# The first 36 products of q in a gated attention/MLP kernel: 128 rows at once, or 64 and 64

## The chip, the cores and the metric

The kernel runs on one core of one Trainium2 chip, in one launch. The metric is the device time of that launch in microseconds (us); three runs of the kernel before gave a median of 392.82 us.

## The reference

For 2048 positions x of width 448 the reference adds two branches, weighted by a gate of each position. One branch is a dilated sliding attention (16 heads of 28, the current position and seven earlier ones at a distance of 2, 4, ... 14); the other is an MLP with a squared ReLU.

```
g   = sigmoid((x * gate_w).sum(-1))
qkv = x @ wqkv                                   # 2048x448 @ 448x1344
a   = attention(q, k, v; 8 positions, step 2) @ wo
h   = relu(x @ w1 + b1) ** 2                     # 448 -> 1792
b   = h @ w2 + b2                                # 1792 -> 448
out = g * a + (1 - g) * b
```

## The kernel before

Everything comes in as float32. The products are made in the format F32R: each matrix is split into a high part (a copy in that format, by ScalarE as a rule) and a low part (the difference, by VectorE as a rule), and each product is made three times: high by high, high by low, low by high. In the names, `wqh` and `wql` are the two parts of the weights of q, k and v, and `x.h[k]` and `x.l[k]` those of the input; k counts three blocks of 128 of the 448 contracted rows. The remaining 64 rows have tiles of their own: `x.x7` and `x.x8` are the high and the low part of the input there, `w7h` and `w7l` those of the weights.

The input comes in four chunks of 512 positions, each of four tiles of 128. A tile of q is an accumulator of 128x450 in one bank of PSUM (448 columns, and two for the gate). The tile of x is the stationary operand of a product, so each product has a weight load (PEld) of 128 columns and a matmul (PE) of 450 columns.

Nearly all products of the kernel are made in **pairs with 64 rows each** by `side_by_side` (line 351): of two products with different accumulators, one takes rows 0 to 63 of both operands and the other rows 64 to 127, and the two run at the same time. An accumulator receives both halves of its products, first in one half of the rows and later in the other. The kernel never lets two products in different halves run on one accumulator at the same time: each change of half is preceded by a tiny write of another engine (`turn`, `touch`): the write waits for the last product in the old half, and the first product in the new half waits for the write.

The exception is the beginning. `qkv_first` works on the four tiles of q of chunk 0 (`q[0]` to `q[3]`) while the input still arrives. There the 3 blocks x 3 products x 4 tiles = 36 products (line 439) use all 128 rows at once and need no turn. Each product is issued when its operands are due: block 0 goes by tiles (0, 1), then (2, 3), since x's first block arrives in two halves of 256 columns; blocks 1 and 2 go by all four tiles. Then follow the products of q with 64 rows (`last`), in pairs with those of the first tiles of k, and everything after them is pairs.

The order of each engine is fixed when the program is built: a planner (`Plan`) keeps a clock of TensorE and places the jobs of ScalarE, VectorE, GpSimd and SyncE's DMA queue by their costs and dependencies. The splits of the first operands (lines 846 to 861) are written out by hand ahead of it, and GpSimd has nothing to do there: after some small fills of constants it is idle until the attention begins.

Of the kernel before, what the change touches and what calls it, by code (L numbers as in the profile page):

```python
# [14 lines left out]
P = 128  # L15
# [8 lines left out]
NQ = D + 2  # L24
# [160 lines left out]
def gated_mix_kernel(ctx: ExitStack, tc: tile.TileContext, xT, wqkv, w1, w2, wo, b1, b2, out):  # L185
    nc = tc.nc

    def f32(ap):
        return ap.bitcast(F32)

    def woven(w):

        if w.shape[1] in (NQ, NQ + 1):
            n = NH if w.shape[1] == NQ else D // 2
            return bass.AP(tensor=w.tensor, offset=w.offset, ap=[list(w.ap)[0], [1, n], [NG, 2]])
        return w.rearrange("p (i n) -> p n i", i=2)
# [9 lines left out]
    def woven_out(pt, n):  # L206
        return (pt[:, :2 * NH] if n == NQ else pt[:, :n]).rearrange("p (n i) -> p n i", i=2)
# [85 lines left out]
    def x_tiles(c):  # L293
        if c % 2:
            x_place[0] = xpool.tile([P, 8 * CH + 16], F32R, tag="x", name=f"x{c}")
            return [x_slot(j, 0 if c == 1 else 16) for j in range(4)]
        return [xap.tile([P, 2, CH], F32R, tag=f"x{j}", name=f"x{c}_{j}") for j in range(4)]
# [28 lines left out]
    def block(b):  # L326
        o = (0, NP, NP + D)[b]
        return slice(o, o + ncols(b))
# [66 lines left out]
    def wqj(b, k):  # L395
        return wq_jobs.get((b, k), ())

    def full(x, acc, tl, b, ks=range(3)):
        sl, n = slice(tl * P, tl * P + P), block(b)
        r = []  # L400
        for k in ks:
            (wh, wl), (xh, xl) = wqj(b, k) or (None, None), x.parts[k] or (None, None)
            r += [(acc, x.h[k][:, sl], wqh[:, k, n], *filter(None, (wh, xh))),
                  (acc, x.h[k][:, sl], wql[:, k, n], *filter(None, (wl,))),
                  (acc, x.l[k][:, sl], wqh[:, k, n], *filter(None, (xl,)))]
        return r

    def last(x, acc, tl, b):
        sl = slice(tl * P, tl * P + P)
        n = block(1) if b == 2 else slice(0, NQ + b)  # L410
        h, l = w7h[:, n], w7l[:, n]
        (wh, wl), (xh, xl) = (wqj(2, 3) if b == 2 else ()) or (None, None), x.parts[3] or (None, None)
        return [(acc, x.x7[:, sl], h, *filter(None, (wh, xh))), (acc, x.x7[:, sl], l, *filter(None, (wl,))),
                (acc, x.x8[:, sl], h, *filter(None, (xl,)))]

    def accs(c, b, tls, tags):
        return [Acc(t, f"qkv{c}_{tl}_{b}", ncols(b)) for t, tl in zip(tags, tls)]

    def run(c, todo, steps):
        a = 0  # L420
        for e, done, *turns in steps:
            side_by_side(todo[0][a:e], todo[1][a:e])
            a = e
            for t in turns:
                t() if callable(t) else turn(*t)
            for b, tl, acc in done:
                assert acc.todo == 0
                qkv_evacuate(acc, c, tl, b)

    def qkv_first(x):  # L430
        four = range(4)
        q = accs(0, 0, four, "bbbb")
        for k in range(3):
            todo = [full(x, q[i], i, 0, (k,)) for i in four]
            for some in ((0, 1), (2, 3)) if k == 0 else (four,):
                for j in range(3):
                    for i in some:
                        acc, a, w, *_ = todo[i][j]
                        nc.tensor.matmul(woven_out(acc.pt, NQ), a, woven(w), start=k == j == 0, stop=False)  # L439
            plan.pe(FIRST[k])  # L440
        for acc in q:
            acc.todo = 3
        k = accs(0, 1, four, "mmmm")
        t = [sum((last(x, a[i], i, b) for i in four), []) for b, a in ((0, q), (1, k))]
        f = [full(x, k[i], i, 1) for i in four]
        run(0, [t[0] + f[0] + f[1] + f[2] + f[3], t[1] + f[2] + f[3] + f[0] + f[1]],
            [(3, [(0, 0, q[0])], (k[0], k[0])),
             (12, [(0, i, q[i]) for i in (1, 2, 3)], (k[1], k[1])),
             (24, [], (k[0], k[2])), (33, [], (k[1], k[3])),
             (39, [(1, 0, k[0]), (1, 2, k[2])]), (48, [(1, 1, k[1]), (1, 3, k[3])])])  # L450
        v = accs(0, 2, four, "bbbb")
        f, l = [full(x, v[i], i, 2) for i in four], [last(x, v[i], i, 2) for i in four]
        run(0, [f[0] + l[0] + f[2] + l[2] + f[1] + f[3], f[1] + l[1] + f[3] + l[3] + f[0] + f[2]],
            [(15, [], (v[0], v[1])), (24, [], (v[2], v[3])),
             (33, [(2, 0, v[0]), (2, 1, v[1])]), (42, [(2, 2, v[2]), (2, 3, v[3])])])
# [386 lines left out]
    x = X(x_tiles(0))  # L842
# [88 lines left out]
    for c in range(4):  # L931
        x = xs[c]
        plan.emit(*(p[0] for p in x.parts if p))
        if c == 0:
            qkv_first(x)
        else:
            qkv_two(x, c, 0)
            if c == 1:
                end = plan.t + 63 * MM448
                plan.quiet = end - 500.0, end + QUIET  # L940
            qkv_two(x, c, 2, (mlp_one, mlp_two) if c == 3 else ())
        chunk_done(c)
# [298 lines left out]
    rows = wo_d.rearrange("(i b) n -> i b n", b=14)  # L1241
# [31 lines left out]
    for g in range(2, 2 * NF):  # L1273
        i, f = g // (NF // 2), g % (NF // 2) * 2
# [3 lines left out]
        last = g == 2 * NF - 1  # L1278
        if not f:
            x, slots = X([nxt[j][0] for j in range(4)]), [nxt[j][1] for j in range(4)]  # L1280
# [105 lines left out]
```

## Time and profile before

| | |
|---|---|
| median of three runs | 392.82 us (392.77 to 393.04) |
| the profiled execution, its own time | 392.98 us |
| its span in the profile | 391.0 us (so 1.98 us lie around it) |
| PE, busy share of the span | 99% |
| DVE, ACT, POOL | 68%, 53%, 67% |
| granted TensorE clock | 1.00 |

PE is TensorE's matmul, PEld its weight load, DVE VectorE, ACT ScalarE, POOL GpSimd and SP the queue that issues most DMAs. An instruction's row in the timeline gives its start and length in us; rows that follow each other on one line of the kernel are merged, and xN says how many there are. A matmul's length holds its way through the array, so successive matmuls overlap: the distance between starts is what a product costs in a stream. In a pair the two starts are a few ns apart.

### The profile page before, as it was taken

Reading aid. Unit: us, or ns where it says so; the run is one execution under the profiler, and the core shown is the slowest. Engines: PE = TensorE matmul, PEld = TensorE weight load, DVE = VectorE, ACT = ScalarE, POOL = GpSimd, SP = SyncE. Lnnn points to the kernel's source line nnn. Section 1 sums busy time; section 2 is a strip of 40 time slices with the busy share of each in tenths; the row PEclk is TensorE's granted clock in tenths of the full one; section 3 lists DMA queues with packets and bytes.
Section 4 is the critical chain, followed back from the end, with each engine's and each line's share of the span. In section 5 each row is a group of like instructions: output and inputs, shape, how many; then the busy total and the mean of one; then the engine's idle time right before and its main releaser. Section 6 shows DMA issues by size and latency. Waiting matters only on the chain.

```text
span 391.0 us, 9281 instructions
## 1 busy us (share of the span) xinstructions
PE 386.6 (99%) x3828; PEld 381.2 (97%) x3828; DVE 267.5 (68%) x356; ACT 205.6 (53%) x501; POOL 260.5 (67%) x165
## 2 busy tenths in 40 slices
PE   9999999999999999999999999999999999999996
PEld 8999999999999999999999999999999999999995
DVE  4525522588686778878866999789767686668454
ACT  4757866362566666445555445345716343456740
POOL 0000002988999989869899987999997979661000
PEclk9999999999999999999999999999999999999999
DMA  7999999997174062644203779745645120226835
GB/s 234 398 360 308 368 377 337 375 383 254 49 246 157 1 219 80 220 171 161 90 2 135 241 190 292 224 109 138 173 153 171 80 96 2 88 62 166 147 101 189
DMA packets 64842, 73.75 MB, mean 189 GB/s; under 512 B 32481, under 2 KB 57633, under 8 KB 64417
## 3 DMA queue, kind: packets, MB, share of 16 engines
q1 hardware_dynamic: 64368, 72.79, 57.2%
q8 instruction: 30, 0.49, 0.5%
q10 hardware_dynamic: 432, 0.38, 0.3%
q14 instruction: 12, 0.09, 0.1%
HBM read 45.71 MB, written 28.25 MB: 189 GB/s over the span
## 4 chain that ended last, share of the span: by engine, by line
PE 99%; DVE 0%; DVEq 0%; issue 0%
PE b L351 33%; PE h L351 32%; PE qkv L351 23%; PE a L351 7%; PE qkv L439 2%; PE warm L820 1%; PE a L1176 1%; DVE bt_b L1057 0%; DVEq L1381 0%
## 5 line engine op out<-in xcount | busy, mean ns | idle before, releaser
L549 POOL TENSOR_TENSOR pp<-q,k 128x896 f32<-128x896 f32 x56 | 116.7, 2119 | 77.2 <-DMA k<-k_d 64.7
L561 POOL TENSOR_TENSOR pp<-lg,v 128x896 f32<-128x896 f32 x64 | 113.8, 1868 | 7.4 <-DVE o L571 3.7
L351 PE MATMUL h<-x,w1h 64*128 64x512 f32 x672 | 114.3, 376 | 0.0
L351 PE MATMUL qkv<-wqh,x 64*128 64x448 f32 (+1 forms) x528 | 82.2, 349 | 0.0
L553 DVE TENSOR_REDUCE lg<-pp 128x32 f32<-128x896 f32 x64 | 66.9, 1076 | 13.4 <-POOL pp L549 13.2
L351 PEld LDWEIGHTS h<-x,w1h 64*128 64x128 f32 x672 | 70.9, 186 | 2.3
L806 DVE TENSOR_TENSOR h<-h,h 128x512 fp32r<-128x512 f32 x56 | 38.6, 689 | 46.7 <-ACT h L805 46.5
L571 DVE TENSOR_REDUCE o<-pp 128x112 f32<-128x896 f32 x64 | 67.8, 1070 | 0.2 <-POOL pp L561 0.2
L351 PE MATMUL h<-x,w1l 64*128 64x512 f32 x336 | 67.6, 376 | 0.0
L351 PE MATMUL b<-w2bh,h 64*128 64x448 f32 x448 | 66.6, 349 | 0.0
L351 PE MATMUL b<-w2ah,h 64*128 64x448 f32 x448 | 66.5, 349 | 0.0
L351 PEld LDWEIGHTS qkv<-wqh,x 64*128 64x128 f32 x528 | 57.3, 186 | 0.0
L802 ACT ACTIVATE h<-h,b1z 128x512 f32<-128x512 f32 x56 | 36.7, 655 | 36.8 <-PE h L351 36.8
L351 PE MATMUL qkv<-wql,x 64*128 64x448 f32 (+1 forms) x264 | 53.4, 349 | 0.0
L351 PEld LDWEIGHTS b<-w2ah,h 64*128 64x128 f32 x448 | 46.5, 193 | 0.2
L351 PEld LDWEIGHTS b<-w2bh,h 64*128 64x128 f32 x448 | 46.4, 193 | 0.2
L351 PE MATMUL b<-w2al,h 64*128 64x448 f32 x224 | 41.9, 349 | 0.0
L351 PE MATMUL b<-w2bl,h 64*128 64x448 f32 x224 | 41.9, 349 | 0.0
L351 PEld LDWEIGHTS h<-x,w1l 64*128 64x128 f32 x336 | 35.6, 186 | 1.0
L804 ACT ACTIVATE h<-h 128x512 fp32r<-128x512 f32 x56 | 33.5, 598 | 1.6
L373 ACT ACTIVATE st<-qkv 128x448 f32<-128x448 f32 x48 | 24.4, 540 | 17.1 <-PE qkv L351 12.5
L805 ACT ACTIVATE h<-h 128x512 f32<-128x512 f32 x56 | 33.2, 592 | 0.0
(112 smaller groups left out, 542.8 us busy)
## 6 DMA issues: line engine op xcount, KB each, us to landing
v<-v_d SPq DMA_DIRECT2D x8, 840.0 KB, 6.1
x_d<-x SPq DMA_DIRECT2D x12, 512.0 KB, 7.7
x<-x_d SPq DMA_DIRECT2D x12, 512.0 KB, 3.7
k<-k_d SPq DMA_DIRECT2D x7, 840.0 KB, 7.0
q_d<-st SPq DMA_DIRECT2D x8, 448.0 KB, 6.5
k_d<-st SPq DMA_DIRECT2D x8, 448.0 KB, 6.1
v_d<-st SPq DMA_DIRECT2D x8, 448.0 KB, 6.6
o_d<-o SPq DMA_DIRECT2D x16, 224.0 KB, 2.2
```

The source lines that it names most:

```text
L351: nc.tensor.matmul(woven_out(acc.pt, acc.n), a[rows], woven(w[rows]), start=acc.todo == acc.all, stop=acc.todo == 1)
L373: nc.scalar.activation(st[0][:, :, t % 2].rearrange("p (i g) c -> p i g c", i=2), unwoven(pt[:, :D]).rearrange("p i (g c) -> p i g c", c=C ...
L439: nc.tensor.matmul(woven_out(acc.pt, NQ), a, woven(w), start=k == j == 0, stop=False)
L549: nc.gpsimd.tensor_mul(pr.rearrange("p (w c) -> p w c", w=W), q[:, s:s + 1].to_broadcast([P, W, C]), k[:, s:s + W])
L553: nc.vector.tensor_reduce(lgs[i][:, s], pr.rearrange("p (w h d) -> p w h d", w=W, h=HG), axis=AX.X, op=ALU.add)
L561: nc.gpsimd.tensor_mul(pr.rearrange("p (h d w) -> p w h d", h=HG, w=W), lgs[i][:, s][:, :, :, None].to_broadcast([P, W, HG, DH]), vs[i][:, ...
L571: nc.vector.tensor_reduce(o_t[par, s][:, g * C:(g + 1) * C], pr.rearrange("p (c w) -> p c w", w=W), axis=AX.X, op=ALU.add)
L802: a = add(ACT, 656.0, lambda pt=pt, r=r: nc.scalar.activation(pt, pt, AF.Relu, bias=b1t[:, f + r:f + r + 1]), ready, *bias_job[:2], prio=NEXT)
L804: b = add(ACT, 600.0, lambda pt=pt, hh=hh: nc.scalar.activation(hh, pt, AF.Square), a, prio=NEXT)
L805: a = add(ACT, 600.0, lambda pt=pt: nc.scalar.activation(pt, pt, AF.Square), b, prio=NEXT)
L806: low = add(DVE, 690.0, lambda pt=pt, hh=hh, hl=hl: nc.vector.tensor_sub(hl, pt, f32(hh)), a, prio=NEXT)
L820: nc.tensor.matmul(warm[:, :2 * P].rearrange("p (i n) -> p i n", i=2), zero, zeros, start=True, stop=True)
```

## The change

The 36 products with 128 rows become 36 pairs with 64 rows. For each block k, a first pass makes the three products of tiles (0, 1), then those of (2, 3), each product on one half of its rows; a second pass does the same with the other halves, beginning with the product of `x.l[k]`. `r` says which half a tile is in: neighbours are in different halves, a tile changes between the passes, and from one block to the next it stays.

Between the passes GpSimd copies two columns of `x.l[k]` onto themselves (one of each tile), for tiles (0, 1) and for (2, 3): the copy waits for the first pass's products of these tiles, and the second pass waits for the copy. After the second pass of block 2 it does the same with `x.h[2]` and then `x.x8`. These are ten copies of 128x2. Since q's tiles 1 and 3 end in the half that `last` uses, they come first there, each with the product of `x.x8` ahead of the other two; q's tiles so finish in the order 1, 0, 3, 2.

```diff
         for k in range(3):
             todo = [full(x, q[i], i, 0, (k,)) for i in four]
-            for some in ((0, 1), (2, 3)) if k == 0 else (four,):
-                for j in range(3):
-                    for i in some:
-                        acc, a, w, *_ = todo[i][j]
-                        nc.tensor.matmul(woven_out(acc.pt, NQ), a, woven(w), start=k == j == 0, stop=False)
+            for second in (False, True):
+                for some in ((0, 1), (2, 3)):
+                    for j in (2, 0, 1) if second else (0, 1, 2):
+                        for i in some:
+                            acc, a, w, *_ = todo[i][j]
+                            r = (i + k + second) % 2
+                            rows = slice(r * 64, r * 64 + 64)
+                            nc.tensor.matmul(woven_out(acc.pt, NQ), a[rows], woven(w[rows]), start=k == j == 0 and not second, stop=False)
+                    if not second or k == 2:
+                        for l in (x.h[k], x.x8) if second else (x.l[k],):
+                            t = l.rearrange("p (t n) -> p t n", n=P)[:, some[0]:some[0] + 2, 0:1]
+                            nc.gpsimd.tensor_copy(t, f32(t))
             plan.pe(FIRST[k])
...
-        t = [sum((last(x, a[i], i, b) for i in four), []) for b, a in ((0, q), (1, k))]
+        t = [sum((last(x, a[i], i, b) for i in o), []) for b, a, o in ((0, q, (1, 0, 3, 2)), (1, k, four))]
+        t[0] = sum((t[0][i + 2:i + 3] + t[0][i:i + 2] for i in range(0, 12, 3)), [])
...
-            [(3, [(0, 0, q[0])], (k[0], k[0])),
-             (12, [(0, i, q[i]) for i in (1, 2, 3)], (k[1], k[1])),
+            [(3, [(0, 1, q[1])], (k[0], k[0])),
+             (12, [(0, i, q[i]) for i in (0, 3, 2)], (k[1], k[1])),
```

On TensorE's queue, the program before has the following rows at the place where block 0 ends and block 1 begins; `qkv_2_0` is tile 2 of q, `x_0` and `x_1` are the tiles of x of blocks 0 and 1 (both parts), and the words in brackets name the engines that a row waits for.

```order
L439 MATMUL qkv_2_0_197<-wqh,x_0_171 128x450 [waits DVE_49]
L439 MATMUL qkv_3_0_198<-wqh,x_0_171 128x450
L439 MATMUL qkv_0_0_195<-wqh,x_1_172 128x450 [waits Activation_49]
L439 MATMUL qkv_1_0_196<-wqh,x_1_172 128x450
L439 MATMUL qkv_2_0_197<-wqh,x_1_172 128x450
```

In the changed program the same two products of `x_0` are followed by the second pass of block 0, and block 1 comes behind it.

```order
L442 MATMUL qkv_2_0_197<-wqh,x_0_171 128x450 [waits DVE_49]
L442 MATMUL qkv_3_0_198<-wqh,x_0_171 128x450
L442 MATMUL qkv_0_0_195<-wqh,x_0_171 128x450 [waits Pool_49]
L442 MATMUL qkv_1_0_196<-wqh,x_0_171 128x450
L442 MATMUL qkv_0_0_195<-wqh,x_0_171 128x450
L442 MATMUL qkv_1_0_196<-wqh,x_0_171 128x450
L442 MATMUL qkv_0_0_195<-wql,x_0_171 128x450
L442 MATMUL qkv_1_0_196<-wql,x_0_171 128x450
L442 MATMUL qkv_2_0_197<-wqh,x_0_171 128x450 [waits Pool_49]
```

What moved is the beginning of block 1, by six pairs; two new waits for GpSimd stand ahead of it.

GpSimd's queue gets these rows, between the fills of constants and the attention; `x_2` is the tile of block 2 and `x_3` that of the last 64 rows.

```order
L446 CAST x_0_171<-x_0_171 128x2 [waits DVE_49,PE_49] x2
L446 CAST x_1_172<-x_1_172 128x2 [waits DVE_49,PE_49]
L446 CAST x_1_172<-x_1_172 128x2 [waits PE_49]
L446 CAST x_2_173<-x_2_173 128x2 [waits DVE_49,PE_49]
L446 CAST x_2_173<-x_2_173 128x2 [waits PE_49]
L446 CAST x_2_173<-x_2_173 128x2 [waits PE_49,Activation_49]
L446 CAST x_3_174<-x_3_174 128x2 [waits DVE_49]
L446 CAST x_2_173<-x_2_173 128x2 [waits PE_49]
L446 CAST x_3_174<-x_3_174 128x2
```

Nothing else of GpSimd moved. On ScalarE, VectorE and SP the instructions stand as before, apart from q's tiles, which leave PSUM in the order 1, 3, 0, 2 where it was 0, 2, 1, 3.

## The prediction, made before the changed kernel ran

> **What bounds the kernel now.** I read the page first (busy time, then the chain that ended last), then TensorE's waits:
>
> ```profile
> PE 386.6 (99%) x3828; PEld 381.2 (97%) x3828; DVE 267.5 (68%) x356; ACT 205.6 (53%) x501; POOL 260.5 (67%) x165
> PE 99%; DVE 0%; DVEq 0%; issue 0%
> PE b L351 33%; PE h L351 32%; PE qkv L351 23%; PE a L351 7%; PE qkv L439 2%; PE warm L820 1%; PE a L1176 1%; DVE bt_b L1057 0%; DVEq L1381 0%
> ...
> PE warm L820 <- PEq L1378: 0.8, 1, 0.8
> ```
>
> The chain is 99% TensorE, and its only wait is for the start of the program. So the end moves by what the start of the stream of products moves, one to one: what the changed 2% (L439) loses or gains stands at the end. What follows shows how tight that part is, first TensorE itself:
>
> ```profile
> 4.95 1.05 PE L439 MATMUL qkv<-wqh,x 128*128 128x450 f32 x2
> 5.83 0.56 PE L439 MATMUL qkv<-wql,x 128*128 128x450 f32 x2
> 6.22 0.92 PE L439 MATMUL qkv<-wqh,x 128*128 128x450 f32 x4
> ...
> 12.11 0.35 PE L439 MATMUL qkv<-wqh,x 128*128 128x450 f32 x1
> 12.39 0.46 PE L351 MATMUL qkv<-w7h,x 64*128 64x450 f32 x2
> ...
> 12.69 0.35 PE L351 MATMUL qkv<-w7l,x 64*128 64x450 f32 x2
> 12.88 0.54 PE L351 MATMUL qkv<-w7h,x 64*128 64x450 f32 x4
> ```
>
> From the fifth product (6.22) to the 36th (12.11) there are 31 distances in 5.89 us: 0.19 each. Pairs with 64 rows also come every 0.19 (12.69 to 12.88). So 36 products cost as much as 36 pairs. Two things are lost beside that. The first products are slow: three by 5.83, about 0.37 each. And at the change from 128 to 64 rows the next pair should start at 12.11 + 0.19 = 12.30, but the second one stands at 12.69, as if the first had run from 12.50: 0.20 lost. I take 12.50 as the true start of that pair (below: the 37th).
>
> The operands come from VectorE (low parts) and ScalarE:
>
> ```profile
> 4.72 0.69 DVE L853 TENSOR_TENSOR wql<-wqraw,wqh 128x225 fp32r<-128x225 f32 x2
> 5.32 0.42 DVE L857 TENSOR_TENSOR x<-xraw,x 128x256 fp32r<-128x256 f32 x1
> 6.07 0.43 DVE L857 TENSOR_TENSOR x<-xraw,x 128x256 fp32r<-128x256 f32 x1 [0.33 <-ACT x L856]
> 6.54 0.63 DVE L847 TENSOR_TENSOR wql<-wqraw,wqh 128x450 fp32r<-128x450 f32 x1
> 7.08 0.68 DVE L857 TENSOR_TENSOR x<-xraw,x 128x512 fp32r<-128x512 f32 x1
> 7.69 0.62 DVE L847 TENSOR_TENSOR wql<-wqraw,wqh 128x450 fp32r<-128x450 f32 x1
> 8.66 0.69 DVE L857 TENSOR_TENSOR x<-xraw,x 128x512 fp32r<-128x512 f32 x1 [0.35 <-ACT x L856]
> 9.82 0.63 DVE L859 TENSOR_TENSOR w7l<-wqraw,w7h 128x450 fp32r<-128x450 f32 x1 [0.47 <-ACT w7h L858]
> 10.64 0.69 DVE L861 TENSOR_TENSOR x<-xraw,x 128x512 fp32r<-128x512 f32 x1 [0.19 <-ACT x L860]
> 11.25 1.74 DVE L269 TENSOR_TENSOR wql<-wqraw,wqh 128x448 fp32r<-128x448 f32 x3
> ...
> 5.62 0.42 ACT L856 ACTIVATE x<-xraw 128x256 fp32r<-128x256 f32 x1 [0.91 <-DMA xraw<-xT]
> ```
>
> **The change, part by part.** *The drain.* The change from 128 to 64 rows moves from 12.3 to the first product, where TensorE waits for operands anyway: at most 0.20 gained.
>
> *Operands that are due earlier.* How soon does a product follow the write of its operand? A cast, the weight load of the first product, and that of the 37th pair:
>
> ```profile
> 4.52 0.28 DVE L851 CAST x<-xraw 128x256 fp32r<-128x256 f32 x1
> ...
> 4.92 0.50 PEld L439 LDWEIGHTS qkv<-wqh,x 128*128 128x128 f32 x2 [0.25 <-ACT wqh L849]
> 12.39 0.19 PEld L351 LDWEIGHTS qkv<-w7h,x 64*128 64x128 f32 x2 [0.28 <-ACT wqh L266]
> ```
>
> The weight load of 4.92 starts 0.12 after the cast's end (4.80), with two waits; and behind the load of 12.39 the pair's true start (12.50) is 0.11 later. I take 0.09 + 0.11 = 0.20. The first pair stays at about 5.1 and the second at 5.5. Pair 3 needs x.l[0]'s first half (5.74): 5.94. Pair 4 needs x.h[0]'s second half (ScalarE, 6.04): 6.24. Pair 6 needs x.l[0]'s second half (6.50): 6.70. Before, these came as the 5th, 7th and 11th product and cost no wait. Pair 7 can start at 6.89, and with no further wait pair 37 at 6.89 + 30 x 0.19 = 12.59, against 12.50. So the drain's 0.20 is given back whole to later operands: **+0.09**, and 0.00 would need a reaction 0.1 quicker.
>
> *The GpSimd copies, if they were alone.* How soon does one follow? Rows:
>
> ```profile
> 13.30 0.16 ACT L358 ACTIVATE qkv<-b1z 1x1 f32<-1x1 f32 x1 [0.96 <-PE qkv L351]
> ...
> L251 POOL MEMSET mask<- x7: 88/91/94, 0.9 to 1.2; 1x7 f32 x1, 1x6 f32 x1, 1x5 f32 x1, 1x4 f32 x1
> ...
> L249 POOL MEMSET mask<- x1: 152/152/152, 0.7 to 0.7; 128x64 f32 x1
> ...
> L598 POOL TENSOR_TENSOR lg<-lg,mask x8: 633/656/678, 93.0 to 321.7; 128x256 f32<-128x256 f32 x8
> ```
>
> ScalarE's touch starts at 13.30, 0.07 after the third pair ended (12.88 + 0.35); I take 0.07 for GpSimd. A copy of 2 elements is bounded by 0.09 (a fill of 7) and 0.66 (256 elements, two inputs); it is nearest to the fills, and I take 0.12. The last pair of a group of three runs 0.35; then 0.07 + 0.12, then 0.20 to the next product: 0.74, against the 0.76 that the three pairs of the other tiles and itself give. So alone the copies just fit; each 0.1 more would cost about 0.1 at four places (three blocks and the end).
>
> *The GpSimd copies beside VectorE.* They are not alone. Where GpSimd worked and VectorE subtracted two SBUF tensors, this is what stands there:
>
> ```profile
> 80.42 8.18 DVE L711 TENSOR_TENSOR w2al<-w2raw,w2ah 128x1792 fp32r<-128x1792 f32 x1 [0.83 <-ACT w2ah L709]
> 89.53 1.54 DVE L711 TENSOR_TENSOR w2al<-w2raw,w2ah 128x1344 fp32r<-128x1344 f32 x1
> ...
> 78.44 4.16 POOL L549 TENSOR_TENSOR pp<-q,k 128x896 f32<-128x896 f32 x2
> 82.56 4.16 POOL L549 TENSOR_TENSOR pp<-qk 128x896 f32<-128x896 f32 x2
> 89.68 3.36 POOL L549 TENSOR_TENSOR pp<-qk 128x896 f32<-128x896 f32 x1 [2.96 <-DVE lg L553]
> ```
>
> A POOL product alone takes about 2.10 (4.16 for two that overlap a little). The one at 89.68 took 3.36 and ended at 93.04; less 2.10, it really began at 90.94, 0.13 before the end of VectorE's subtraction (89.53 + 1.54 = 91.07). And VectorE's subtraction of 80.42 stood 8.18 us until GpSimd's run was over. So the two exclude each other, whole instruction by whole instruction. In the window of the change VectorE does nothing but such subtractions, with few gaps. Walking it through, with the lock free 0.13 before a subtraction's end:
> - Block 0, tiles (0, 1): pair 3 ends at 6.29; the copy is due at 6.36, and the subtraction of 6.07 lets go at 6.37: 6.49, no loss.
> - Block 0, tiles (2, 3): pair 6 ends at 7.05, due at 7.12, but the subtraction of 7.08 has it until 7.64. Copy done at 7.76, pair 10 at 7.96 instead of 7.46: **+0.50**.
> - Block 1: pair 15 ends at 9.26, copied by 9.45 in the gap before 9.82, no loss. Pair 18 ends at 9.83, due at 9.90, and 9.82 holds it until 10.32: pair 22 at 10.64 instead of 10.24, **+0.40**.
> - Block 2: pair 27 ends at 11.94, due at 12.01; the second of the three subtractions (about 11.79 to 12.41) holds it until 12.28: pair 31 at 12.60 instead of 12.35, **+0.25**. The second copy waits for the third of them: **+0.05**.
> - The last copies (x.h[2], then x.x8) follow at 13.40 with VectorE idle: two in a row, **+0.05**. VectorE's next block hangs on ScalarE behind a touch that waits for pair 39, so it moves along.
>
> Sum: 0.09 + 0.50 + 0.40 + 0.25 + 0.05 + 0.05 = **1.34 us**. Against the profiled execution's own time: 392.98 + 1.34 = 394.32; that execution lies 0.16 above the median, so 392.82 + 1.34 = **394.2**.
>
> Here a rule can be set beside the row of 8.18. The Trainium skill, "SBUF — State Buffer", section "Who interferes with whom", says that a GpSimd instruction that reads SBUF and a VectorE instruction with two SBUF inputs contend, and that whichever issues first holds the port for its whole instruction. By it, one subtraction is waited for, and the sum stays as above. The row says more: VectorE was passed over between three successive GpSimd instructions. If that holds the other way round, it is the first rival.
>
> *VectorE's own delay* by the copies is at most 0.12 each, and the products that need its operands come later than that; nothing. *q's other order:* three tiles are evacuated after the same steps as before; nothing. SP's stores of x now also wait for the copies, and what is queued behind them would be held up; but the first of them comes ten us after the last copy (about 14):
>
> ```profile
> 23.70 3.26 SPq L885 DMA_DIRECT2D x_d<-x  x3
> ```
>
> So nothing. From there on every engine follows TensorE's stream, so they move along by the same amount.
>
> **The rivals.**
> 1. *GpSimd is passed over between back-to-back subtractions*, as VectorE was. Then the copy due at 7.12 waits out 7.08 and 7.69 (until 8.31 - 0.13 = 8.18): pair 10 at 8.50, +1.04. The later stalls shift: +0.43 at block 1 (until 10.32), +0.26 at block 2, +0.10 at the end. Sum with 0.09: 1.92, so 394.7. For it: the row of 8.18. Against it: no row shows GpSimd passed over; at 89.68 it got in behind one subtraction.
> 2. *No exclusion for so small a copy, so no slower:* two elements slip in, the copies fit in 0.76, and only the operands' +0.09 stays: 392.9. It holds as long as a copy comes out of GpSimd within 0.14 of its start. For it: nothing but the size. Against it: 89.68 waited before it did any work.
> 3. *Quicker reactions and the drain saved*: pair 3 at 5.83 and no wait after it: pair 37 at 5.83 + 34 x 0.19 = 12.29, a gain of 0.21: 392.6. Against it: x.l[0] ends at 5.74 and 6.50.
> 4. *Something dearer*: a copy of 0.3 or more on top of the exclusion adds 0.2 at four places and makes 395 and above.
>
> **How the numbers follow.** A measurement of this kernel can tell about 0.2%, 0.79 us, from no change: the bounds are 392.0 and 393.6. Forecast 0.47 (1.0 to 1.7 with the luck of who comes first at 7.1, 9.8 and 12.0); rival 1 0.22, rival 2 0.24, rival 3 0.03, rival 4 0.04. Slower by over 0.2%: 0.47 + 0.22 + 0.04 = 0.73. Within: 0.24 + 0.02 = 0.26. Faster by that much: 0.01, as even rival 3 stays inside. The range reaches from rival 2 (392.9) past rival 1 (394.7), with 0.2 for unknown lengths of a copy: 392.9 to 394.9.
>
> **What would show it.** In the changed profile: pairs 4 and 6 near 6.2 and 6.7; a hole of about 0.5 in TensorE's starts between 7.3 and 8.0 (of 1.0 for rival 1), another near 10.3 and 12.5; TensorE waiting for POOL at L442; POOL's copies of 0.1, but of 0.4 to 0.6 where VectorE subtracts; the first pair of `last` at 13.8 instead of 12.5; and from there all as before, shifted by 1.3. It is wrong if the copies run at 0.1 to 0.15 beside VectorE's subtractions, or if TensorE's shift at 14 us is not the shift at the end.

## The result, and the profile after

| | before | changed |
|---|---|---|
| median of six runs each, same chip | 392.88 us | 394.75 us (394.64 to 395.05) |
| ratio | | 1.0049, 95% interval 1.0036 to 1.0062 |
| profiled execution, own time / span | 392.98 / 391.0 us | 394.64 / 392.8 us |

The change made the kernel 1.87 us slower. The forecast was 394.2 with a range of 392.9 to 394.9; a second comparison of the same two kernels on another chip (below) gave 1.50.

The page of the changed kernel: busy time, and the chain that ended last.

```profile
PE 387.6 (99%) x3864; PEld 375.5 (96%) x3864; DVE 266.1 (68%) x356; ACT 205.7 (52%) x501; POOL 264.9 (67%) x175
PE 97%; DMA 2%; POOL 0%; DVE 0%; DVEq 0%; issue 0%
```

TensorE still carries it, but 2% of the chain is now a DMA (the chain counts the 6.26 us of the whole transfer; the wait for it is shorter), and that was in no part of the prediction. First the part that was changed. TensorE in the timeline, start and length in us; what is cut out is products in even steps:

```profile
6.46 0.35 PE L442 MATMUL qkv<-wql,x 64*128 64x450 f32 x2
...
7.30 0.35 PE L442 MATMUL qkv<-wql,x 64*128 64x450 f32 x2
7.94 0.65 PE L442 MATMUL qkv<-wqh,x 64*128 64x450 f32 x4 [0.29 <-POOL x L446]
8.43 0.35 PE L442 MATMUL qkv<-wql,x 64*128 64x450 f32 x2
...
11.67 0.35 PE L442 MATMUL qkv<-wql,x 64*128 64x450 f32 x2
11.86 0.91 PE L442 MATMUL qkv<-wqh,x 64*128 64x450 f32 x6
12.60 0.35 PE L442 MATMUL qkv<-wql,x 64*128 64x450 f32 x2
12.79 0.62 PE L442 MATMUL qkv<-wqh,x 64*128 64x450 f32 x4
13.25 0.35 PE L442 MATMUL qkv<-wql,x 64*128 64x450 f32 x2
13.46 0.64 PE L351 MATMUL qkv<-w7h,x 64*128 64x450 f32 x3
13.76 0.54 PE L351 MATMUL qkv<-w7l,x 64*128 64x448 f32 x2
```

Each group of three pairs has one row with `wql`, which serves as a mark. From pair 9 (7.30) to pair 12 (8.43) are three steps, 0.57 at 0.19 each; they took 1.13: 0.56 lost at pair 10, which waits for POOL. From pair 29 (11.67) to pair 33 (12.60) are four steps, and 0.17 was lost; from 33 to 36 (13.25) 0.08; from 36 to 38 (13.76) 0.13. Between pair 12 and pair 29 there is no loss: 8.43 to 11.67 are 17 steps of 0.19 (and 0.01). The row of a pair that had to wait begins about 0.1 too early, so its true start is taken as one step before that of the next pair. For pair 37 this is 13.76 - 0.19 = 13.57, against 12.50.

GpSimd's ten copies in the same execution, and VectorE's subtractions beside the second, third and fifth:

```profile
6.49 0.19 POOL L446 CAST x<-x 128x2 fp32r<-128x2 f32 x1 [5.09 <-PE qkv L442]
7.16 0.73 POOL L446 CAST x<-x 128x2 fp32r<-128x2 f32 x1 [0.48 <-PE qkv L442]
9.42 0.19 POOL L446 CAST x<-x 128x2 fp32r<-128x2 f32 x1 [1.53 <-PE qkv L442]
9.99 0.19 POOL L446 CAST x<-x 128x2 fp32r<-128x2 f32 x1 [0.38 <-PE qkv L442]
11.72 0.35 POOL L446 CAST x<-x 128x2 fp32r<-128x2 f32 x1 [1.53 <-PE qkv L442]
12.29 0.43 POOL L446 CAST x<-x 128x2 fp32r<-128x2 f32 x1 [0.22 <-PE qkv L442]
13.10 0.31 POOL L446 CAST x<-x 128x2 fp32r<-128x2 f32 x2 [0.38 <-PE qkv L442]
...
7.16 0.68 DVE L865 TENSOR_TENSOR x<-xraw,x 128x512 fp32r<-128x512 f32 x1
7.79 0.63 DVE L855 TENSOR_TENSOR wql<-wqraw,wqh 128x450 fp32r<-128x450 f32 x1
...
9.43 0.66 DVE L867 TENSOR_TENSOR w7l<-wqraw,w7h 128x450 fp32r<-128x450 f32 x1
...
11.39 1.84 DVE L269 TENSOR_TENSOR wql<-wqraw,wqh 128x448 fp32r<-128x448 f32 x3
```

A copy that waits for nobody is 0.19 long. The one at 7.16 began together with a subtraction of 0.68 and took 0.73. If 0.19 of this is its own, it waited 0.54, and VectorE let go at 7.70, 0.14 before the end of its record (7.84). The next subtraction stood ready (7.79), and the copy did not wait for it: it was done at 7.89, and that subtraction ended at 8.42. The subtraction was hardly held up: it starts 0.63 behind the one before it, and 0.61 behind it in the kernel before.

The second loss is 150 us later. TensorE's timeline there, of the kernel before and then of the changed one:

```profile
161.17 0.63 PE L351 MATMUL h<-x,w1h 64*128 64x512 f32 x4
...
162.68 0.39 PE L351 MATMUL b<-w2bh,h 64*128 64x448 f32 x2
```

```profile
162.24 0.63 PE L351 MATMUL h<-x,w1h 64*128 64x512 f32 x4
...
163.64 0.48 PE L351 MATMUL h<-x,w1h 64*128 64x512 f32 x2 [0.34 <-DMA x<-x_d]
...
164.39 0.35 PE L351 MATMUL b<-w2bh,h 64*128 64x448 f32 x2
```

Here the MLP waits for a block of x that is loaded again. Ahead of this wait TensorE is 1.07 later than in the kernel before (162.24 against 161.17), behind it 1.71 (164.39 against 162.68). So some 0.65 of this execution's loss came from a transfer. A small rest stands at the very end: from the start of the last matmul to the end of the span the changed kernel takes 4.12 to 4.13 us in its three profiles, and the kernel before 3.98 to 4.01 in its three. It is 4.11 with fills in the place of the copies too, so the copies are not its cause; what is, stays open.

### The profile page after: what moved, and what is told of

Read it like the earlier page. It is cut to its first block, busy times and chain, and to the rows that moved or that the text cites. A ratio compares the mean times of both kernels' runs of the same rounds, so it can differ in the third digit from the quotient of the medians.

```text
span 392.8 us, 9371 instructions
## 1 busy us (share of the span) xinstructions
PE 387.6 (99%) x3864; PEld 375.5 (96%) x3864; DVE 266.1 (68%) x356; ACT 205.7 (52%) x501; POOL 264.9 (67%) x175
## 4 chain that ended last, share of the span: by engine, by line
PE 97%; DMA 2%; POOL 0%; DVE 0%; DVEq 0%; issue 0%
PE h L351 32%; PE b L351 31%; PE qkv L351 23%; PE a L351 7%; PE qkv L442 2%; DMA x<-x_d 2%; PE warm L828 1%; PE a L1184 1%; POOL x L446 0%; DVE bt_b L1065 0%; DVEq L1389 0%
## 5 line engine op out<-in xcount | busy, mean ns | idle before, releaser
L557 POOL TENSOR_TENSOR pp<-q,k 128x896 f32<-128x896 f32 x56 | 118.3, 2140 | 67.1 <-DMA k<-k_d 53.9
L351 PE MATMUL h<-x,w1h 64*128 64x512 f32 x672 | 112.1, 376 | 0.3 <-DMA x<-x_d 0.3
L351 PEld LDWEIGHTS h<-x,w1h 64*128 64x128 f32 x672 | 67.5, 186 | 5.7 <-DMA x<-x_d 0.7
L351 PE MATMUL h<-x,w1l 64*128 64x512 f32 x336 | 65.8, 376 | 0.0
L351 PE MATMUL b<-w2ah,h 64*128 64x448 f32 x448 | 65.3, 349 | 0.0
L351 PE MATMUL b<-w2bh,h 64*128 64x448 f32 x448 | 65.3, 349 | 0.0
L351 PEld LDWEIGHTS b<-w2ah,h 64*128 64x128 f32 x448 | 45.0, 192 | 0.5
L351 PEld LDWEIGHTS b<-w2bh,h 64*128 64x128 f32 x448 | 44.7, 193 | 0.5
L351 PE MATMUL b<-w2bl,h 64*128 64x448 f32 x224 | 40.6, 349 | 0.0
L351 PEld LDWEIGHTS h<-x,w1l 64*128 64x128 f32 x336 | 33.8, 186 | 2.2
```

Of the source, the lines that this page charges most:

```text
L351: nc.tensor.matmul(woven_out(acc.pt, acc.n), a[rows], woven(w[rows]), start=acc.todo == acc.all, stop=acc.todo == 1)
L557: nc.gpsimd.tensor_mul(pr.rearrange("p (w c) -> p w c", w=W), q[:, s:s + 1].to_broadcast([P, W, C]), k[:, s:s + W])
```

## The experiments

The open points were: are the holes the exclusion of GpSimd by VectorE, the copies' own length, or the pairs; and does the wait at 163 us belong to the change. All comparisons are with the kernel before on the same chip.

**Ten products of zeros behind the 36, in the kernel before** (a pure delay):

```diff
             plan.pe(FIRST[k])
+        for _ in range(10):
+            nc.tensor.matmul(warm[:, :2 * P].rearrange("p (i n) -> p i n", i=2), zero, zeros, start=True, stop=True)
```

> The kernel before with ten more products of zeros (128x256, into the warm-up's bank) behind the 36 products with 128 rows: at 0.107 us each TensorE's stream is 1.07 us later from 12.3 us on, as much as in the changed kernel, and nothing else is touched. The theory that the later wait of 0.65 us for the second reload of x (at 163 us) comes of the shift by itself: that wait shows again, 392.9 + 1.07 + 0.65 = 394.6. The rival that it belongs to the changed kernel (its other order of stores, GpSimd's copies) or to chance: no wait there, 394.0.

394.18 against 393.20 us, ratio 1.0029 (1.0017 to 1.0040). The added time reaches the end, and there is no wait for x's reload: in that profile the stream was 1.45 later at 16 us than in the first profile of before, and 1.45 at the end. So a later stream alone did not bring the wait at 163 us in this profile.

**Each tile in one half throughout, no copies of x.l:**

```diff
-                            r = (i + k + second) % 2
+                            r = (i + 1) % 2
...
-                    if not second or k == 2:
+                    if second and k == 2:
```

> The changed kernel with each tile of q in the same half in both passes, so that no copy of x.l is needed; those of x.h[2] and x.x8 at the end stay. Half of each product's rows are left out (the other half counted twice), the work of TensorE is the same. The theory that GpSimd's copies behind VectorE's subtractions are what stalls TensorE: the holes at 7.9, 12.1 and 12.8 us go, what stays is the earlier need of operands (0.1) and the last copies (0.1): the first pair of the last 64 rows at 12.7, in all 393.1. The rival that the pairs themselves, or their operands, cost it: holes stay, over 393.7.

393.54 against 393.20, ratio 1.0010 (1.0001 to 1.0019). From pair 3 to pair 36 no step is longer than 0.19 in its trace, so the pairs themselves cost nothing. The expectation put this kernel 0.2 above the kernel before, and it is 0.34 above. One place in its trace costs far more than the 0.1 that was written for it. GpSimd and VectorE there, then TensorE:

```profile
12.26 1.51 POOL L446 CAST x<-x 128x2 fp32r<-128x2 f32 x4 [10.87 <-PE qkv L442]
...
11.72 1.76 DVE L269 TENSOR_TENSOR wql<-wqraw,wqh 128x448 fp32r<-128x448 f32 x3
...
12.41 0.35 PE L442 MATMUL qkv<-wql,x 64*128 64x450 f32 x2
13.58 0.65 PE L351 MATMUL qkv<-w7h,x 64*128 64x450 f32 x3 [0.82 <-POOL x L446]
```

TensorE comes sooner to the last four copies, and these now fall among the three subtractions of 11.72 to 13.48: pair 37 is 1.09 late. Taking away the earlier stalls moved the later one into VectorE's way. (In this execution 0.3 of it was regained at the end: 3.67 us from the last matmul's start, against 3.98 in the first profile of before.)

**Fills that read nothing in the place of the copies:**

```diff
-                            nc.gpsimd.tensor_copy(t, f32(t))
+                            nc.gpsimd.memset(f32(t), 0.0)
```

> The changed kernel with each copy on GpSimd replaced by a fill with zeros of the same two columns, which writes there but reads nothing from SBUF (so the first column of each tile is zero in the second pass). The theory that the two engines exclude each other in reading two SBUF operands: the fills take 0.1 each wherever they fall and never wait for a subtraction; the stalls of 0.93 go, 393.1. The rival that any GpSimd instruction is kept out by a subtraction: 0.4 to 0.7 for the second fill as before, 394.7.

393.28 against 393.20, ratio 1.0008 (0.9999 to 1.0017): no difference that can be told. The second, sixth, seventh and eighth of the ten fills, and VectorE beside the last three:

```profile
7.23 0.11 POOL L446 MEMSET x<- 128x2 f32 x1 [0.80 <-PE qkv L442]
...
11.79 0.10 POOL L446 MEMSET x<- 128x2 f32 x1 [0.47 <-PE qkv L442]
12.43 0.13 POOL L446 MEMSET x<- 128x2 f32 x2 [0.53 <-PE qkv L442]
...
11.29 1.85 DVE L269 TENSOR_TENSOR wql<-wqraw,wqh 128x448 fp32r<-128x448 f32 x3
```

None waits: that of 7.23 started with a subtraction of 0.68 (0.01 ahead of it), as the copies of 0.73 did, and the three others lie inside a row of three subtractions (11.29 to 13.14). From pair 7 to pair 37 TensorE takes 5.71 us here, 30 steps of 0.19: no stall, and no drain either.

**Fills as long as a copy:**

```diff
-                            t = l.rearrange("p (t n) -> p t n", n=P)[:, some[0]:some[0] + 2, 0:1]
-                            nc.gpsimd.tensor_copy(t, f32(t))
+                            t = l.rearrange("p (t n) -> p t n", n=P)[:, some[0]:some[0] + 2, 0:56]
+                            nc.gpsimd.memset(f32(t), 0.0)
```

> As the kernel with fills of two columns, but each fill covers 56 columns in each of the two tiles (112 elements; zeros are left there), which makes it about 0.19 long, as long as a copy that doesn't wait (fills of 2 took 0.10 and one of 64 took 0.15). It reads nothing. The theory that the loss is copies kept out by VectorE: no fill waits, 0.05 over the slack of 0.14 at about four places, 0.1 to 0.4 over the kernel before. The rival that the length of a copy, 0.19 where 0.12 was taken, is the larger part: 0.8 or more over the kernel before.

393.70 against 392.97, ratio 1.0016 (1.0007 to 1.0025): more than the theory gave, less than the rival. In the trace:

```profile
7.53 0.20 POOL L446 MEMSET x<- 128x112 f32 x1 [0.60 <-PE qkv L442]
...
12.75 0.32 POOL L446 MEMSET x<- 128x112 f32 x2 [0.45 <-PE qkv L442]
```

No fill waits. The length itself costs 0.02 at pair 10 and 0.20 at pair 37, where two follow each other (0.32); the rest of this profile's lateness is operands (pairs 4 and 6 lost 0.45), the slow first products, and 0.2 at 112 us, where TensorE waits for VectorE. So with 0.19 of length and no exclusion the stalls between pair 7 and pair 37 sum to 0.23, where the copies make 0.9 to 1.3.

**VectorE with one operand:** each of its subtractions there replaced by a copy, as in

```diff
-            nc.vector.tensor_sub(wl, raw, f32(wh))
+            nc.vector.tensor_copy(wl, raw)
```

> The changed kernel with each subtraction of VectorE in that stretch (the low parts of x and of the weights of q, k and v in chunk 0) replaced by a copy of the raw operand, which reads one SBUF tensor instead of two (so these low parts are the raw values). GpSimd's copies stay as they are. The theory that it is VectorE's second SBUF operand that keeps GpSimd out: all ten copies take 0.19 and none waits, the holes of 0.56, 0.17 and 0.08 go, 393.3 to 393.5. The rival that any VectorE instruction on SBUF keeps a reading GpSimd out: some copies still take 0.3 to 0.7, 394.2 or more.

393.58 against 393.34, ratio 1.0008 (0.9999 to 1.0017). The time is as the theory had it, but the reason fails: GpSimd's copies still waited.

```profile
6.00 0.40 POOL L446 CAST x<-x 128x2 fp32r<-128x2 f32 x1 [4.62 <-PE qkv L442]
7.14 0.41 POOL L446 CAST x<-x 128x2 fp32r<-128x2 f32 x1 [0.73 <-PE qkv L442]
...
5.97 0.39 DVE L855 CAST wql<-wqraw 128x450 fp32r<-128x450 f32 x1
7.11 0.40 DVE L855 CAST wql<-wqraw 128x450 fp32r<-128x450 f32 x1 [0.24 <-DMA wqraw<-wqkv]
```

These copies of VectorE take 0.39 to 0.40 for 450 columns, where the subtraction takes 0.63, and they keep GpSimd out for about 0.22. So a second operand is not the only way to exclude it, and this run does not isolate it (the Trainium skill, "SBUF — State Buffer", "Who interferes with whom", says that a copy on VectorE can take both ports and then excludes GpSimd as well, which agrees with the 0.40 and 0.41). The stall at pair 10 fell from 0.56 to 0.24, as VectorE's instructions are shorter, but in this profile 0.17 in block 1 and 0.39 at pair 37 came beside it, 0.81 in all, hardly less than in the changed kernel. The low parts were also ready sooner (pair 3 starts at 5.57 where it started at 6.05), so the better time is not evidence on the exclusion.

**Each copy twice:**

```diff
-                            nc.gpsimd.tensor_copy(t, f32(t))
+                            for _ in range(2):
+                                nc.gpsimd.tensor_copy(t, f32(t))
```

> The changed kernel with each copy of GpSimd made twice in a row. A second copy starts 0.125 behind the first (13.10 and 13.22 in the changed kernel's trace). The theory that a copy's own length is a small part of the loss and the waiting for subtractions the large one: 0.1 more at each of four to six places, some of it hidden, and a second copy that falls behind the next subtraction waits 0.6 once or twice: 395.1 to 395.9. The rival that the copies' own length makes the stalls: six times 0.19 and more, with no copy longer than 0.2 that was not so before, 395.8 and above with even holes.

396.67 against 393.34, ratio 1.0098 (1.0081 to 1.0116): above the theory's range. It lies where the rival had it (395.8 and above), but the rival's other sign, no copy longer than 0.2 that was not so before, fails. GpSimd's four copies of block 0 and the eight of the end:

```profile
6.77 1.80 POOL L447 CAST x<-x 128x2 fp32r<-128x2 f32 x4 [5.38 <-PE qkv L442]
...
14.53 1.55 POOL L447 CAST x<-x 128x2 fp32r<-128x2 f32 x8 [0.46 <-PE qkv L442]
```

Two things were mis-sized: a copy that follows one of the same columns starts 0.25 behind it, not 0.125 (it waits for it), and three of the four in block 0 met a subtraction (0.42, 0.54 and 0.60 long). So length and exclusion are not two separate sums here: the longer a chain of copies is, the more subtractions it can meet.

**The groups in another order,** so that most copies have 1.33 instead of 0.76:

```diff
-            for second in (False, True):
-                for some in ((0, 1), (2, 3)):
+        steps = [(0, 0, 0), (0, 0, 2)]
+        for k in range(3):
+            for some in (0, 2):
+                steps += [(k, 1, some)] + ([(k + 1, 0, some)] if k < 2 else [])
+        for k, second, s in steps:
```

> The changed kernel with the groups of three pairs in another order: the first pass of the next block for tiles (0, 1) stands ahead of the second pass of this block for tiles (2, 3), and so on, so that a copy has 1.33 us where it had 0.76, except for the first one and the last group. Operands, copies and halves are the same. The theory that the stalls are copies kept out by subtractions beyond a slack of 0.76: the hole at 7.9 goes (its copy still takes 0.7), about 0.13 for x.l of block 1 comes, and what remains is a hole of 0.2 to 0.5 in the last group near 12.2, 393.6 to 394.1. The rival that more changes of order only move the loss: 394.7 as before.

394.14 against 393.34, ratio 1.0024 (1.0015 to 1.0033), in the theory's direction, 0.04 above its range. The copy that made the hole of 0.56 is as long as before, and its pair does not wait:

```profile
7.55 0.74 POOL L449 CAST x<-x 128x2 fp32r<-128x2 f32 x1 [1.00 <-PE qkv L445]
```

The stalls behind pair 7 are 0.13 (pair 12, for x.l of block 1), 0.07 and 0.13. The time is 0.80 above the kernel before, about half of the changed kernel's loss. In this profile pair 4 also waited 0.54 for the second half of x's first block.

**Both kernels again, for what varies.**

> The changed kernel once more, for what varies. Both theories: 394.7, the second copy 0.6 to 0.75 long. The stalls in block 1 depend on when VectorE's next operands arrive: if the last 64 rows of the weights land 0.4 later, as in the profile of before, block 1 stalls by 0.4 too. If the wait for x's reload at 163 us is chance, it is gone here; if it comes of the shift, it is there again with 0.5 to 0.8.

> The changed kernel for a third profile. The first pair of the last 64 rows between 13.5 and 14.2, one copy of 0.6 to 0.75 near 7.3; the wait for x's reload at 163 us shows in one of its two profiles so far and in none of four others: if chance, it is more likely absent.

> The kernel before once more, for a second profile. By both theories 392.6 to 393.6, and no wait for GpSimd; it shows how much the arrival of the first operands moves the first pair of the last 64 rows (12.50 in the first profile) from one execution to the next: by 0.3 or less if the difference between the kernels is to be read from single profiles.

> The kernel before for a third profile: the first pair of the last 64 rows between 12.2 and 12.8, no wait later.

The changed kernel on the second chip: 394.70 against 393.20, ratio 1.0040 (1.0026 to 1.0053); a single run on the third, with the third profile, took 394.31, where the kernel before has 392.97. The second copy of block 0, then (in the next two rows) the second copy of block 1 and the subtraction beside it, then the copies of block 2, in the second profile and in the third:

```profile
7.46 0.73 POOL L446 CAST x<-x 128x2 fp32r<-128x2 f32 x1 [0.87 <-PE qkv L442]
...
10.30 0.19 POOL L446 CAST x<-x 128x2 fp32r<-128x2 f32 x1 [0.38 <-PE qkv L442]
9.79 0.63 DVE L867 TENSOR_TENSOR w7l<-wqraw,w7h 128x450 fp32r<-128x450 f32 x1
...
12.03 0.78 POOL L446 CAST x<-x 128x2 fp32r<-128x2 f32 x2 [1.53 <-PE qkv L442]
```

```profile
7.33 0.73 POOL L446 CAST x<-x 128x2 fp32r<-128x2 f32 x1 [0.46 <-PE qkv L442]
...
10.17 0.20 POOL L446 CAST x<-x 128x2 fp32r<-128x2 f32 x1 [0.38 <-PE qkv L442]
9.70 0.63 DVE L867 TENSOR_TENSOR w7l<-wqraw,w7h 128x450 fp32r<-128x450 f32 x1
...
11.90 0.30 POOL L446 CAST x<-x 128x2 fp32r<-128x2 f32 x1 [1.53 <-PE qkv L442]
12.47 0.28 POOL L446 CAST x<-x 128x2 fp32r<-128x2 f32 x1 [0.27 <-PE qkv L442]
```

The stalls of the three profiles of the changed kernel, and where pair 37 truly starts:

| | pair 4, 6 | pair 10 | block 1 | block 2 | pair 37 | start of pair 37 |
|---|---|---|---|---|---|---|
| first | 0.11 | 0.56 | 0.01 | 0.25 | 0.13 | 13.57 |
| second | 0.49 | 0.56 | 0.01 | 0.48 | 0.20 | 14.19 |
| third | 0.25 | 0.56 | 0.02 | 0.12 | 0.20 | 13.71 |

In the kernel before pair 37 starts at 12.50, 12.28 and 13.02 in three profiles: the operands of the first product land up to 0.4 later (12.91 below), and the slow first products are one to three. How long TensorE stays slow also differs: the 18 warm-up products ahead of q come every 0.21 us to the last in eleven of the thirteen profiles, but in those of the fills and of VectorE with one operand their step falls to 0.11 from the 14th or 15th on.

```profile
12.17 0.46 PE L351 MATMUL qkv<-w7h,x 64*128 64x450 f32 x2
```

```profile
12.91 0.46 PE L351 MATMUL qkv<-w7h,x 64*128 64x450 f32 x2
...
PEld b L351 <- DVE h L806: 0.5, 1, 0.5
```

The mean difference between the two kernels at pair 37 is 1.22. The spread of 0.74 for one kernel is well above the 0.3 that was asked for if single profiles were to be compared, and as large as single terms of the prediction, so that terms are read from steps within a profile and not from starts. The wait for x at 163 us is in one of the three profiles of the changed kernel (and 0.2 of it where the copies were made twice), in none of those with a delay alone, with fills, with one half or with more slack. The third profile of the kernel before, which was expected to have no late wait, has one of another kind (0.4 at 111 us, TensorE for VectorE; last row), and the long fills have 0.2 of that. So such waits come and go with an execution. Whether the changed kernel has the one at 163 us more often is left open.

## Why the prediction was right, and where it was not

**That TensorE's stream decides, one to one:** right, and shown by the pure delay. But "from there all as before" did not hold in the first profile: TensorE was 1.07 later at 14 us and 1.67 at the last matmul, which the prediction had named a sign of being wrong. The path is right; that no transfer would come into it was assumed. The second and third profiles keep their shifts (1.69 and 1.21) to the end.

**The drain:** right. In the kernel before, the step into pair 37 is 0.20 too long in all three profiles, in the kernel with fills there is none.

**Operands due earlier (the +0.09 is 0.29 against the drain's 0.20):** the mechanism was right and the size is not one number. By the walk pairs 4 and 6 lose 0.19 (0.11 and 0.08); they lost 0.11, 0.49 and 0.25 in the three profiles, the more the later the second half of x's first block landed. Pair 7 so starts at 6.92, 7.23 and 7.10, where 6.89 was written.

**The exclusion:** right in kind. Fills of the same place and time lose nothing (0.08 in the median), copies 1.5 to 1.9. The term of **+0.50** at pair 10 came out at 0.56 in all three profiles; the copy alone is 0.07 longer than was taken. That it must be VectorE's second operand that keeps a copy out is not shown: VectorE's own copies did it too.

**Block 1, +0.40: wrong.** It was 0.01 to 0.02. The step that failed is who comes first there: the walk had the fourth copy due at 9.90, early in a subtraction that starts at 9.82 in the one profile of before. In the first profile of the changed kernel that subtraction started earlier (9.43). In the other two it started nearly as written (9.79 and 9.70), but TensorE was later and the copy was due at 10.30 and 10.17. In all three the third copy came just ahead of the subtraction, and the fourth 0.10 to 0.16 before its end, when VectorE was letting go. The prediction had named this place as luck, and it was. **Block 2, +0.30:** 0.25, 0.48 and 0.12, by the same luck.

**The copy's length:** 0.19 where 0.12 was taken from the fills. A fill of two columns did take 0.10; a copy also reads. **The end, +0.05:** 0.13 to 0.20, since two copies of 0.19 follow each other there; the long fills, which wait for nobody, lose 0.20 there.

So where 1.25 was written for the stalls, they came to 0.94, 1.26 and 0.90. In the first profile pair 37 was only 1.07 later, less than the forecast 1.34, and the execution took 394.64 against the forecast 394.32 because of the 0.65 at 163 us and the longer end. In the second it was late operands and block 2. The range held both. That the number came out close is in part luck: the missing 0.40 of block 1 and what came later offset each other. On average the traces account for 1.22 at pair 37 and 0.13 at the end, 1.35 in all. The comparisons gave 1.87, 1.50 and (from a single run) 1.34, and what the first two have beyond 1.35 stays open: one profile in three shows a late wait.

**Rival 1** (passed over between subtractions) fell: with one subtraction ending at 7.84 and the next ready, the copy waited for the first alone. The Trainium skill's rule that was weighed there ("SBUF — State Buffer", "Who interferes with whom"), by which whoever issues first holds the port for its whole instruction, agrees with the 0.54 of waiting beside a subtraction of 0.68. The 8.18 us of before, read the other way round, would have given 1.04 at pair 10 and not 0.56. **Rival 2** (no exclusion) did not happen to the copies; the fills are what it would have looked like. The same section of the Trainium skill says that a VectorE instruction with two SBUF inputs does not contend with a GpSimd instruction that only writes, and the 0.11 at 7.23 agrees. **Rival 3** did not show. **Rival 4** (copies of 0.3 or more on top of the exclusion) did not happen either, as a copy takes 0.19; the doubled copies show what it would cost, at 396.67.

## What to carry to other kernels

A tiny instruction on an idle engine is not free if a busy engine can keep it out, as VectorE did with GpSimd's copies here (0.73 instead of 0.19): price it by the longest instruction of the other engine, and see whether the place leaves that much time. If only an order is wanted, a write that reads nothing avoided it here (0.08 in the median), and more products between the write and its reader avoided about half of it (0.80 was lost in place of 1.5 to 1.9). Such a write must go where its value does no harm: the fills here overwrote columns of the input. And where a walk through a few us rests on the arrival of DMAs, take two or three profiles before adding up who comes first.

## What the runs showed of the hardware that was not expected

- A GpSimd copy of 128x2 takes 0.19 us, as long as a fill of 128x112 (0.19 to 0.20); a fill of 128x2 takes 0.10.
- A VectorE copy from float32 of 128x450 takes 0.39 to 0.40 (0.63 for the subtraction) and keeps GpSimd's copies out too (0.40 and 0.41 instead of 0.19).
- A second GpSimd copy starts 0.25 behind the first if it has the same columns, and 0.12 if it has others.
- Between executions of one kernel the start of the 37th pair varied by 0.7 us (12.28 to 13.02), by the landing of the first DMAs and by how many of the first products were slow. When the slow ones end differs: in two of thirteen profiles the step of the warm-up's products had already fallen from 0.21 to 0.11.
